# Decay attention in two sub-chunks of 64 tokens: every attention product as 64x64 tiles of the array

## The chip, the cores and the metric

The kernel runs on one core of one Trainium2 chip. The metric is the time of one execution on the device in microseconds (us), the median of several. The engines are named as in the profile: PE is TensorE (its weight loads are PEld), DVE is VectorE, ACT is ScalarE, POOL is GpSimd, SP is SyncE, which here only issues DMAs.

## The reference

Attention with a decaying state, then two feed-forward layers; all inputs are float32, and only the attention matters here.

```python
def _attn_ref(q, k, v, lam):          # q, k, v: 2 x 8 heads x 768 tokens x 64
    block = 64
    Dmask = np.where(rel >= 0, lam[:, None, None] ** rel[None, :, :], 0.0)
    for b in range(nb):
        intra = np.einsum('bhic,bhjc->bhij', qb, kb) * Dmask[None]
        intra = np.einsum('bhij,bhjd->bhid', intra, vb)
        inter = np.einsum('bhid,bhde->bhie', qb * lam_pow[None], kv_state)
        out[:, :, sl] = intra + inter
        kb_dec = kb * rev_pow[None]
        kv_state = lam_block[None, :, None, None] * kv_state + np.einsum('bhsd,bhse->bhde', kb_dec, vb)
...
x = moe(silu(x @ w_gate) * (x @ w_val) @ w_out);  return (g(x @ w_in)) @ w_out2   # 1536 tokens, g(h) = h cos h
```

The block of 64 is a way to compute, not part of the result: with the right powers of lam any block length gives the same numbers.

## The kernel before

A **chunk** is 128 tokens of one batch row with all eight heads; there are 12 (`NCH`), six for each of the two batch rows. Each chunk goes through these steps, which the PE executes in a written order (`steps_of`), mixed with feed-forward work:

- `t`: q and k are transposed on the PE (line 881), four 128x128 products each, and copied by ACT to `qt` and `kt`. The q side is multiplied by powers of lam on POOL to `qd`.
- `s`: the scores (line 895), eight products of 64 rows, 128x128 results. DVE multiplies them by the table `dmask` to `at`.
- `st`: the chunk's share of the state (line 902), eight products over 128 tokens with 64x64 results. DVE adds it to the old state, which POOL has multiplied by a power of lam (`stmp`).
- `av`: scores by values (line 908), eight products over 128 tokens with 64x128 results.
- `qs`: `qd` by the state (line 917), eight 64x64 weights against 128 columns, added into the same PSUM banks as `av`. ACT and DVE turn the sum into `xh` and `xl`, the input of the first layer.

A product of float32 operands (all but `t`) is two MATMUL records in the profile. Line 243 multiplies zeros where the order expects the PE to wait. A **unit** is one product of the first layer for 512 tokens: twelve matmuls of 512 columns on lines 136 to 138. All the matmuls of the feed-forward layers use three terms of split operands (`wh`, `wl`; `xh`, `xl`), for which DVE and ACT convert each loaded weight piece.

No order is left to the hardware: while the program is built, a small planner plays all engines with times written in the kernel (`ATT_NS`, the nanoseconds in `go(...)`), and emits each engine's instructions in the order in which they came up. An engine then executes its list strictly in order. The attention is the first part of the program; `FILL` says in how many places of it the planner should reckon with a unit. When the last chunk's `x` is there, DVE computes sums of `x` blocks (`t1`, `t2`, ..., `u1`, ...) that later products need (Strassen-like products of half blocks). DMAs of q, k, v and of weight pieces are all issued by SP, in the planner's order; a tile has 2 to 5 buffers (`BUFS`), and a load waits until its buffer is free.

Of the kernel before, what the change touches and what calls it, by code (L numbers as in the profile page):

```python
# [9 lines left out]
F32 = mybir.dt.float32  # L10
# [44 lines left out]
def kernel(  # L55
# [25 lines left out]
    C = P  # L81
    NPAIR = H // 2
# [115 lines left out]
    down_d = dram.tile([H, 2 * C], F32, name="down_d")  # L198
    down = att.tile([H, 2 * C], F32, name="down")
    anti = att.tile([P, P], F32, name="anti")  # L200
    dmask = att.tile([P, H, C], F32, name="dmask")
    zeros = att.tile([P, 512], mybir.dt.bfloat16, name="zeros")
    sel = s_tile(0, "sel")[0:H]
    lrow = att.tile([P, NPAIR, C], F32, name="lrow")
    state = [att.tile([P, NPAIR, D], F32, name=f"state{i}") for i in range(2)]

    def att_tile(nm, i):

        shape = {"q": [P, H, D], "k": [P, H, D], "v": [P, H, D], "kd": [P, H, D], "at": [P, H, C], "stmp": [P, NPAIR, D]}
        return att.tile(shape.get(nm, [P, NPAIR, C]), F32, tag=f"{nm}{i}", name=nm)  # L210

    def tables():
# [3 lines left out]
        nc.scalar.dma_start(down[:, C - 1:C], lam.rearrange("(h o) -> h o", o=1))  # L216
        nc.scalar.activation(warm, halfpi, AF.Silu)
        nc.vector.memset(down[:, C + 1:], 0.0)
        nc.vector.memset(down[:, C:C + 1], 1.0)
        n = 1  # L220
        while n < C:
            nc.vector.tensor_scalar(
                out=down[:, C - 2 * n:C - n], in0=down[:, C - n:C],
                scalar1=down[:, C - n:C - n + 1], scalar2=None, op0=ALU.mult,
            )
            n *= 2
        nc.scalar.dma_start(down_d, down)

    def load_mask():

        e = down_d[:, :]
        nc.sync.dma_start(dmask, bass.AP(e.tensor, e.offset + 1, [[1, P], [2 * C, H], [1, C]]))
# [13 lines left out]
    for g in range(NCH):  # L246
        if g % CPB != CPB - 1:
            steps_of.append(("st", g))
        steps_of.append(("av", g))
        if g % CPB:  # L250
            steps_of.append(("qs", g))
        if not g:
            steps_of += [("t", "q", 2), ("t", "k", 2)]
        if g + 2 < NCH:
            steps_of.append(("s", g + 2))
        if g + 3 < NCH:
            steps_of += [("t", "q", g + 3), ("t", "k", g + 3)]
        steps_of += [None] * FILL[g]
# [345 lines left out]
    def fetch(key, i):  # L604

        yield go("SP", 2300 if key[0] in up_w else 1700, lambda: load_piece(key, i))
# [145 lines left out]
    def qkv_job(nm, g):  # L752
# [6 lines left out]
        yield go("SP", 1330, lambda: nc.sync.dma_start(t, src[b, :, c * C:(c + 1) * C, :].rearrange("h p d -> p h d")))  # L759
# [7 lines left out]
    def t_copy_job(nm, g, b, ps):  # L767
# [7 lines left out]
        if nm == "q" and g % CPB:  # L775
# [3 lines left out]
            yield tt(qd[:, :, ::-1], t, lrow, ALU.mult, "POOL")  # L779
# [15 lines left out]
    readers = {}  # L795

    def done(nm, g, t):

        n = readers[nm, g] = readers.get((nm, g), 0) + 1
        if n == (2 if nm in ("k", "v", "qt") and (nm == "qt" and g % CPB or nm != "qt" and g % CPB != CPB - 1) else 1):  # L800
            give(nm, made_att.pop((nm, g))[0], t)

    def tmp_job(g):

        yield "wait", ("state", g)
        i = yield "take", "stmp"
        t = att_tile("stmp", i)
        yield tt(t, state[g % 2], lrow[:, :, 0:1].to_broadcast([P, NPAIR, D]), ALU.mult, "POOL")
        made_att["stmp", g] = i, t
        signal(("stmp", g), (yield "now",))  # L810

    def state_job(g, b, ps):

        pv = ps[:, 0:NPAIR * D].rearrange("p (a e) -> p a e", a=NPAIR)
        new = state[(g + 1) % 2]
        if g % CPB > 1 or g % CPB == 0 and g:
            yield "wait", ("qs", g - 1)
        if g % CPB:
            yield "wait", ("stmp", g)
            yield tt(new, made_att["stmp", g][1], pv, ALU.add, psum=True)  # L820
            done("stmp", g, (yield "now",))
# [3 lines left out]
        signal(("state", g + 1), (yield "now",))  # L825
# [583 lines left out]
```

## Time and profile before

| | |
|---|---|
| median of 3 runs | 597.47 us (597.45 to 597.63) |
| the profiled execution's span | 595.7 us |
| what lies around the span (median less span) | 1.8 us |
| PE busy / DVE busy / ACT busy / POOL busy | 589.6 / 500.8 / 347.9 / 30.5 us |
| attention | from the start to 80.65 us, with 7 units in it |

The span is the time from the first to the last instruction of one profiled execution; the timed runs have no profile and lie 1.8 us above it. The busy time of PE counts overlapping matmuls once, so a PE that is "busy" may still be waiting for its own pipeline: the starts of the groups tell more than their durations.

### The profile page before, as it was taken

How to read it: one execution, taken by the hardware profiler on the slowest of the kernel's cores; microseconds unless marked ns; L12 is line 12 of the kernel's file. 1: busy time of each engine (PE TensorE's matmuls, PEld its weight loads, DVE VectorE, ACT ScalarE, POOL GpSimd, SP SyncE). 2: the span in 40 equal slices, each digit the busy share in tenths (PEclk: the TensorE clock that was granted, in tenths of full speed). 3: DMA queues.
4: the chain of work that ended last, by engine and by line, in shares of the span. 5: the costliest groups of instructions: out<-in, count | busy, mean ns of one | idle time of the engine just before them, and what ended most of it. 6: DMA issues, size and time to landing. Idle time of an engine off the chain costs nothing.

```text
span 595.7 us, 8964 instructions
## 1 busy us (share of the span) xinstructions
PE 589.6 (99%) x3356; PEld 488.4 (82%) x3358; DVE 500.8 (84%) x885; ACT 347.9 (58%) x626; POOL 30.5 (5%) x37
## 2 busy tenths in 40 slices
PE   8999999999999999999999999999999999999997
PEld 5878878888888888888888878888888888888886
DVE  3568789999788788786889999999898999998854
ACT  2455455676656455544543776988666676676620
POOL 3634200000000000000000000000000000000000
PEclk9999999999999999999999999999999999999999
DMA  9999832058536537334322120110101222200005
GB/s 184 204 205 195 197 83 70 2 159 245 165 120 161 150 115 161 126 90 139 105 84 76 37 70 19 53 56 33 31 6 40 69 69 73 70 1 1 0 1 211
DMA packets 70570, 57.72 MB, mean 97 GB/s; under 512 B 39672, under 2 KB 61440, under 8 KB 70528
## 3 DMA queue, kind: packets, MB, share of 16 engines
q1 hardware_dynamic: 70496, 57.16, 36.7%
q8 instruction: 26, 0.43, 0.3%
q14 instruction: 16, 0.13, 0.1%
q10 hardware_dynamic: 32, 0.01, 0.0%
HBM read 49.81 MB, written 7.35 MB: 96 GB/s over the span
## 4 chain that ended last, share of the span: by engine, by line
PE 96%; DVE 3%; ACT 0%; issue 0%; DVEq 0%; ACTq 0%
PE bank L136 24%; PE bank L138 23%; PE bank L137 23%; PE bank L1237 5%; PE bank L1238 5%; PE bank L1239 5%; PE bank L895 2%; PE bank L881 2%; PE bank L908 2%; PE bank L243 1%; PE bank L902 1%; PE bank L917 1%; DVE sum L486 1%; DVE s L486 0%; DVE wl L498 0%
## 5 line engine op out<-in xcount | busy, mean ns | idle before, releaser
L136 PE MATMUL bank<-xl,wh 128*128 128x512 f32 (+1 forms) x336 | 123.5, 368 | 0.0
L137 PE MATMUL bank<-xh,wh 128*128 128x512 f32 (+1 forms) x336 | 122.6, 365 | 0.0
L138 PE MATMUL bank<-xh,wl 128*128 128x512 f32 (+1 forms) x336 | 122.3, 364 | 0.0
L493 ACT ACTIVATE s<-s 128x512 f32<-128x512 f32 (+2 forms) x112 | 65.8, 592 | 47.2 <-DVE s L486 27.4
L493 ACT ACTIVATE s<-bank 128x512 f32<-128x512 f32 (+2 forms) x114 | 61.2, 538 | 52.7 <-PE bank L138 47.3
L493 ACT ACTIVATE gh<-s 128x512 fp32r<-128x512 f32 x84 | 52.8, 629 | 58.3 <-PE bank L1238 30.9
L498 DVE TENSOR_TENSOR wl<-ct,wh 128x512 fp32r<-128x512 f32 x104 | 71.6, 702 | 6.4 <-ACT wh L493 6.3
L493 ACT ACTIVATE wh<-ct 128x512 fp32r<-128x512 f32 x104 | 63.4, 625 | 19.9 <-DVE ct L187 16.2
L137 PE MATMUL bank<-wh,gh 128*128 128x512 f32 (+1 forms) x194 | 75.0, 387 | 0.0
L136 PE MATMUL bank<-wl,gh 128*128 128x512 f32 (+1 forms) x194 | 75.0, 387 | 0.0
L138 PE MATMUL bank<-wh,gl 128*128 128x512 f32 (+1 forms) x194 | 75.0, 387 | 0.0
L136 PEld LDWEIGHTS bank<-xl,wh 128*128 128x128 f32 x336 | 63.3, 188 | 12.0 <-issue 0.7
L486 DVE TENSOR_TENSOR sum<-bank,sum 128x512 f32<-128x512 f32 (+1 forms) x101 | 65.1, 680 | 8.6 <-PE bank L138 7.8
L138 PEld LDWEIGHTS bank<-xh,wl 128*128 128x128 f32 x336 | 63.3, 188 | 10.3
L137 PEld LDWEIGHTS bank<-xh,wh 128*128 128x128 f32 x336 | 63.4, 189 | 10.1
L486 DVE TENSOR_TENSOR gl<-s,gh 128x512 fp32r<-128x512 f32 x84 | 57.8, 689 | 10.5 <-ACT gh L493 10.5
L486 DVE TENSOR_TENSOR s<-bank,s 128x512 f32<-128x512 f32 (+1 forms) x84 | 49.3, 591 | 16.7 <-PE bank L138 16.2
L1238 PE MATMUL bank<-gh,wh 128*128 128x512 f32 x144 | 56.3, 391 | 0.0
L1237 PE MATMUL bank<-gh,wl 128*128 128x512 f32 x144 | 56.3, 391 | 0.0
L1239 PE MATMUL bank<-gl,wh 128*128 128x512 f32 x144 | 56.0, 389 | 0.0
L187 DVE SCALAR_TENSOR_TENSOR ct<-ct,raw 128x512 int32<-128x512 int32 x68 | 46.8, 688 | 3.3 <-ACT ct L175 0.2
L175 ACT ACTIVATE ct<-raw 128x512 f32<-128x512 f32 x68 | 44.8, 663 | 3.7 <-DMA raw<-in_moe_w_out_dram 1.1
(122 smaller groups left out, 950.8 us busy)
## 6 DMA issues: line engine op xcount, KB each, us to landing
raw<-in_moe_w_out_dram SPq DMA_DIRECT2D x28, 512.0 KB, 3.6
raw<-in_moe_w_in_dram SPq DMA_DIRECT2D x16, 512.0 KB, 3.9
raw<-in_moe_w_gate_dram SPq DMA_DIRECT2D x24, 256.0 KB, 4.2
raw<-in_moe_w_val_dram SPq DMA_DIRECT2D x24, 256.0 KB, 4.3
q<-in_q_dram SPq DMA_DIRECT2D x12, 256.0 KB, 5.7
k<-in_k_dram SPq DMA_DIRECT2D x12, 256.0 KB, 5.5
v<-in_v_dram SPq DMA_DIRECT2D x12, 256.0 KB, 5.2
out_dram<-sum SPq DMA_DIRECT2D x11, 256.0 KB, 2.0
```

The lines of the kernel that those rows point to most:

```text
L136: nc.tensor.matmul(ps, wh, xl, start=first, stop=False, **kw)
L137: nc.tensor.matmul(ps, wh, xh, start=False, stop=False, **kw)
L138: nc.tensor.matmul(ps, wl, xh, start=False, stop=last, **kw)
L175: nc.scalar.activation(t, words[:, :, 1].bitcast(F32), AF.Prelu, scale=2.0 ** -112, alpha=2.0 ** 32)
L187: nc.vector.scalar_tensor_tensor(out=w, in0=w, scalar=3, in1=lo, op0=ALU.logical_shift_left, op1=ALU.bitwise_or)
L486: engine, n * (1.18 if engine == "DVE" else 2.45), lambda: unit.tensor_tensor(out=out, in0=in0, in1=in1, op=op),
L493: return go("ACT", 40 + n * 0.94, lambda: nc.scalar.activation(out, src, fn, **kw))
L498: return "any", {"DVE": n * 1.18, "POOL": n * 2.45}, lambda e: (nc.vector if e == "DVE" else nc.gpsimd).tensor_tensor(out=out, in0=in0, in ...
L881: nc.tensor.transpose(ps[:, p * P:(p + 1) * P], src[:, 2 * p:2 * p + 2, :].rearrange("p a d -> p (a d)"), anti if op[1] == "q" else ident,)
L1237: nc.tensor.matmul(ps, lo[:, cs], gh, start=first, stop=False)
L1238: nc.tensor.matmul(ps, hi[:, cs], gh, start=False, stop=False)
L1239: nc.tensor.matmul(ps, hi[:, cs], gl, start=False, stop=last)
```

## The change

A chunk stays 128 tokens for loads, transpositions and the output, but is computed in two sub-chunks `u` of 64 tokens (`CS`). The scores are only computed within a sub-chunk (64x64 results, two to a head), `dmask` and `at` are half as wide. The state is advanced twice a chunk (`st` makes two shares from 64 tokens each, with four state buffers), `qs` is two steps with a state each, and `av` is two steps: in the first each half of the array's rows writes one of the two output banks, in the second the other, with a `drain` of the PE ahead of the second. All of `s`, `st`, `av` and `qs` use 64x64 tiles of the array with 64 columns. The planner's times are changed with it, also those of the loads.

```diff
-ATT_NS = {"t": 480, "spread": 1080, "s": 1100, "st": 530, "av": 1080, "qs": 600}
+ATT_NS = {"t": 520, "spread": 400, "s": 540, "st": 530, "av": 270, "qs": 270}
-BUFS = {"q": 3, "k": 3, "v": 5, "qt": 2, "kt": 2, "qd": 3, "kd": 2, "at": 2, "stmp": 2}
+BUFS = {"q": 3, "k": 3, "v": 5, "qt": 2, "kt": 2, "qd": 3, "kd": 2, "at": 3, "stmp": 2}
+STATES = 4
+DRAIN = 150
...
     for g in range(NCH):
-        if g % CPB != CPB - 1:
-            steps_of.append(("st", g))
-        steps_of.append(("av", g))
-        if g % CPB:
-            steps_of.append(("qs", g))
...
+        steps_of.append(("st", g))
+        if g and g + 1 < NCH:
+            steps_of.append(("s", g + 1))
+        steps_of.append(("av", 0, g))
+        ahead = [2, 3] if not g else [g + 3] if g + 3 < NCH else []
+        steps_of += [("t", "q", n) for n in ahead]
+        steps_of += [("t", "k", n) for n in ahead]
+        steps_of += [None] * FILL[g]
+        steps_of.append(("av", 1, g))
...
-        yield go("SP", 2300 if key[0] in up_w else 1700, lambda: load_piece(key, i))
+        yield go("SP", 1800 if key[0] in up_w else 1700, lambda: load_piece(key, i))
...
-                    for h2, (_, ps) in enumerate(got):
-                        r = slice(64 * h2, 64 * h2 + 64)
-                        nc.tensor.matmul(ps[:, p * C:(p + 1) * C], kt[r, p, :], qt[r, p, :], start=True, stop=True)
+                    for h2 in range(2):
+                        for u in range(2):
+                            nc.tensor.matmul(
+                                got[h2][1][half(u), p * CS:(p + 1) * CS], kt[half(h2), p, half(u)], qt[half(h2), p, half(1 - u)],
+                                start=True, stop=True, skip_group_check=True,
+                            )
...
+                if turn:
+                    nc.tensor.drain()
...
+                for y in range(2):
+                    for u in range(2):
+                        for c in range(2):
+                            f = u ^ 1 ^ turn
+                            h = 2 * (2 * c + y) + f
+                            nc.tensor.matmul(
+                                put(made_att["out", g], f, c, y, u), vn[half(u), h, :], at_[half(u), h, :],
+                                start=not y and not turn, stop=turn == 1, skip_group_check=True,
+                            )
```

How this moves the PE's instructions: first a chunk of the middle of the attention before, where `bank2` and `bank4` are the output banks of chunk 7; steps come as `st`, `av`, `s`, `qs`.

```order
L902 MATMUL bank1_814<-v_414,kd_601 64x64 x8
L908 MATMUL bank2_825<-at_684,v_414 64x128 x4
L908 MATMUL bank4_826<-at_684,v_414 64x128 x4
L895 MATMUL bank5_840<-qt_776,kt_784 128x128
L895 MATMUL bank6_841<-qt_776,kt_784 128x128
```

The same part of the PE's list now, from the last scores of chunk 7 to the second half of `av` of chunk 6 (line 918 is `s`, 943 `av`, 904 `t`; `q_657` and `k_789` are the q and k of chunk 9):

```order
L918 MATMUL bank3_974<-qt_784,kt_795 64x64 x2
L918 MATMUL bank1_975<-qt_784,kt_795 64x64 x2
L943 MATMUL bank5_998<-at_860,v_424 64x64 x2
L943 MATMUL bank6_997<-at_860,v_424 64x64 x2
L904 MATMUL bank0_1010<-anti_89,q_657 128x128 x4
L904 MATMUL bank3_1018<-ident_84,k_789 128x128 x4
L943 MATMUL bank6_997<-at_860,v_424 64x64 x2
L943 MATMUL bank5_998<-at_860,v_424 64x64 x2
```

Every step is of 64x64 tiles, and the transpositions of chunk 9 stand between the two halves of one `av`, directly behind one another.

SP's list of loads, before, from the fifth to the twelfth (`v_142` is the v of chunk 0, `q_146` the q of chunk 2):

```order
L759 DMA v_142<-in_v_dram 128x8x64
L232 DMA dmask_90<-down_d_87 128x8x128
L759 DMA q_146<-in_q_dram 128x8x64
L759 DMA k_147<-in_k_dram 128x8x64
L759 DMA q_161<-in_q_dram 128x8x64
L759 DMA v_145<-in_v_dram 128x8x64
```

And now, from the v of chunk 0 (`v_143`) on, then behind the "..." the loads up to the k of chunk 9:

```order
L765 DMA v_143<-in_v_dram 128x8x64
L765 DMA q_147<-in_q_dram 128x8x64
L236 DMA dmask_90<-down_d_87 64x8x64 x2
L765 DMA q_162<-in_q_dram 128x8x64
...
L765 DMA k_678<-in_k_dram 128x8x64
L765 DMA v_424<-in_v_dram 128x8x64
L765 DMA q_657<-in_q_dram 128x8x64
L157 DMA raw_897<-in_moe_w_val_dram 64x4x256 x2
L765 DMA k_789<-in_k_dram 128x8x64
```

The load of `dmask` (512 KB before, now two of 128 KB) has one more q ahead of it. The four first weight pieces all stand ahead of the k of chunk 9; three did before.

The end of the attention on the PE, before: `av` of chunk 11, a unit (its twelve matmuls go on behind the "..."), `qs`, and the next unit.

```order
L908 MATMUL bank2_1130<-at_1011,v_747 64x128 x4
L136 MATMUL bank0_1144<-xl_135,wh_719 128x512
...
L917 MATMUL bank6_1129<-qd_950,state1_95 64x128
...
L136 MATMUL bank5_1178<-xl_135,wh_811 128x512
```

The unit of `bank0_1144` is the seventh. Now:

```order
L943 MATMUL bank4_1552<-at_1464,v_1038 64x64 x2
L139 MATMUL bank0_1607<-xl_136,wh_1095 128x512
...
L952 MATMUL bank3_1551<-qd_1335,state2_96 64x64 x2
...
L139 MATMUL bank6_1688<-xl_138,wh_595 128x512
```

Here the unit of `bank0_1607` is the eighth: one unit more stands ahead of the last `qs`, and one fewer behind it. Behind that the lists of the feed-forward layers are nearly the same.

## Rows read from the trace of the kernel before

**Rows 1.** The page: busy time and share; the chain that ended last, by engine.

```profile
PE 589.6 (99%) x3356; PEld 488.4 (82%) x3358; DVE 500.8 (84%) x885; ACT 347.9 (58%) x626; POOL 30.5 (5%) x37
...
PE 96%; DVE 3%; ACT 0%; issue 0%; DVEq 0%; ACTq 0%
```

**Rows 2.** Stretches, core 0: length, busy by engine, clock, DMA share, GB/s.

```profile
core 0: us, PE busy (x) PEld busy (x) DVE busy (x) ACT busy (x) POOL busy (x), PEclk, DMA share, GB/s
5.00:63.00 58.00, 57.20 (x719) 45.26 (x720) 34.55 (x63) 25.84 (x53) 27.36 (x27) 1.00 1.11 204
...
90.00:105.00 15.00, 15.00 (x71) 12.53 (x70) 14.70 (x19) 8.39 (x13) 0.00 (x0) 1.00 0.28 70
105.00:120.00 15.00, 15.00 (x82) 12.95 (x81) 14.52 (x26) 10.11 (x20) 0.00 (x0) 1.00 0.01 2
```

**Rows 3.** Waits of PE, 5.7 to 80.7 us: total, times, longest.

```profile
PE bank L895 <- ACT kt L493: 0.6, 2, 0.3
```

**Rows 4.** Timeline of PE, middle of the attention: start, length, line, operands, count.

```profile
39.52 0.66 PE L881 MATMUL bank<-anti,q 128*128 128x128 f32 x4
40.11 1.09 PE L908 MATMUL bank<-at,v 128*64 128x128 f32 x16
41.13 0.66 PE L881 MATMUL bank<-ident,k 128*128 128x128 f32 x4
41.72 0.67 PE L917 MATMUL bank<-qd,state 64*64 64x128 f32 x16
42.32 0.66 PE L881 MATMUL bank<-anti,q 128*128 128x128 f32 x4
42.91 1.16 PE L895 MATMUL bank<-qt,kt 64*128 64x128 f32 x16
44.00 0.66 PE L881 MATMUL bank<-ident,k 128*128 128x128 f32 x4
...
47.33 0.69 PE L902 MATMUL bank<-v,kd 128*64 128x64 f32 x16
47.84 1.05 PE L908 MATMUL bank<-at,v 128*64 128x128 f32 x16
48.82 1.16 PE L895 MATMUL bank<-qt,kt 64*128 64x128 f32 x16
49.91 0.66 PE L881 MATMUL bank<-anti,q 128*128 128x128 f32 x4
50.40 0.60 PE L881 MATMUL bank<-ident,k 128*128 128x128 f32 x4
```

**Rows 5.** One stretch of 0.045 us, line 917 alone: PE busy and records, clock, DMA.

```profile
41.70:41.74 0.04, 0.02 (x4) 1.00 1.20 250
```

**Rows 6.** Timeline of PE: a run of zeros.

```profile
12.53 1.90 PE L243 MATMUL bank<-zeros 128*128 128x512 bf16 x8
14.27 0.60 PE L881 MATMUL bank<-anti,q 128*128 128x128 f32 x4
```

**Rows 7.** Timeline of SP: start and length of a DMA's issue.

```profile
3.70 1.14 SPq L759 DMA_DIRECT2D v<-in_v_dram  x1
7.78 0.37 SPq L232 DMA_DIRECT2D dmask<-down_d  x1
...
41.26 3.13 SPq L759 DMA_DIRECT2D k<-in_k_dram  x1
```

**Rows 8.** Timeline, end of the attention.

```profile
77.11 0.50 PE L136 MATMUL bank<-xl,wh 128*128 128x512 f32 x1
...
80.05 0.67 PE L917 MATMUL bank<-qd,state 64*64 64x128 f32 x16
...
80.65 0.50 PE L136 MATMUL bank<-xl,wh 128*128 128x512 f32 x1
...
81.19 0.76 DVE L486 TENSOR_TENSOR xl<-bank,xh 128x256 fp32r<-128x256 f32 x2
```

**Rows 9.** Timeline behind the attention: a sum's low half, and its first use.

```profile
101.67 1.22 DVE L486 TENSOR_TENSOR t2l<-sum,t2h 128x1024 fp32r<-128x1024 f32 x1
...
103.96 0.39 PE L136 MATMUL bank<-t2l,wh 128*128 128x512 f32 x1
```

**Rows 10.** Groups of POOL and DVE, 0 to 120 us: busy, mean ns | idle before.

```profile
L486 POOL TENSOR_TENSOR qd<-qt,lrow 128x512 f32<-128x512 f32 x10 | 12.9, 1294 | 24.1 <-ACT qt L493 24.1
L486 POOL TENSOR_TENSOR kd<-k,dmask 128x512 f32<-128x512 f32 x10 | 10.5, 1058 | 9.1 <-issue 4.9 <-DMA k<-in_k_dram 3.0 <-DMA dmask<-down_d 1.3
L486 POOL TENSOR_TENSOR stmp<-state,lrow 128x256 f32<-128x256 f32 x8 | 5.9, 733 | 2.4 <-DVE state L486 2.4
```

More of the change, by code (lines that the diff above doesn't have):

```diff
@@ L81 @@
     C = P
+    CS = C // 2
     NPAIR = H // 2
@@ L824, in state_job @@
         drop_bank(b, (yield "now",))
-        signal(("state", g + 1), (yield "now",))
+        signal(("state", n + 1), (yield "now",))
     def at_job(g, got):
@@ L903, in fn @@
             elif kind == "av":
                 at_, vn = made_att["at", g][1], made_att["v", g][1]
-                made_att["out", g] = list(got)
-                for f in range(2):
-                    for a in (0, 2, 1, 3):
-                        nc.tensor.matmul(
-                            put(got, f, a), vn[:, 2 * a + f, :], at_[:, 2 * a + f, :],
-                            start=a % 2 == 0, stop=not g % CPB and a % 2 == 1, skip_group_check=True,
-                        )
+                turn = op[1]
@@ new lines, in fn @@
+                if turn:
+                    nc.tensor.drain()
+                else:
+                    made_att["out", g] = list(got)
+                for y in range(2):
+                    for u in range(2):
+                        for c in range(2):
+                            f = u ^ 1 ^ turn
+                            h = 2 * (2 * c + y) + f
+                            nc.tensor.matmul(
+                                put(made_att["out", g], f, c, y, u), vn[half(u), h, :], at_[half(u), h, :],
+                                start=not y and not turn, stop=turn == 1, skip_group_check=True,
+                            )
@@ L912, in fn @@
             else:
-                out_, qd = made_att["out", g], made_att["qd", g][1]
+                out_, qd, u = made_att["out", g], made_att["qd", g][1], op[1]
                 for y in range(2):
-                    for f, a in ((0, y), (1, y + 2), (0, y + 2), (1, y)):
-                        r = slice(64 * f, 64 * f + 64)
-                        nc.tensor.matmul(
-                            put(out_, f, a), state[g % 2][r, a, :], qd[r, a, :], start=False, stop=y == 1, skip_group_check=True
-                        )
+                    for f in range(2):
+                        for c in range(2):
+                            nc.tensor.matmul(
+                                put(out_, f, c, y, u), state_of(2 * g + u)[half(f), 2 * c + y, :], qd[half(f), 2 * c + y, half(u)],
+                                start=False, stop=y == 1, skip_group_check=True,
+                            )
@@ L935, in then @@
             else:
-                signal((kind, g), t)
-                if kind == "av":
+                signal(op, t)
+                if kind == "qs":
+                    done("qd", g, t)
+                elif op[1]:
                     done("at", g, t)
                     done("v", g, t)
-                else:
-                    done("qd", g, t)
-                if kind == "qs" or not g % CPB:
+                if kind == "qs" and op[1]:
                     for f, (b, ps) in enumerate(made_att["out", g]):
                         spawn(out_job(g, f, b, ps), seen[op], t)
-        return dict(ns=ATT_NS[kind], needs=needs, keys=[], bank=n, fn=fn, then=then, clock=seen[op], op=op)
+        return dict(ns=ATT_NS[kind] + DRAIN * (op[:2] == ("av", 1)), needs=needs, keys=[], bank=n, fn=fn, then=then, clock=seen[op], op=op)
     def open_mlp(t):
@@ L1366 @@
             for nm in "qkv":
[L1367 removed]
+                spawn(qkv_job(nm, g), seen["t", "q", g] if nm == "q" else seen["t", "k", g] if nm == "k" else seen["av", 0, g] - 1)
         spawn(mask_job(), seen["s", 0], 6500)
         for g in range(NCH):
[L1370 to L1373 removed]
+            spawn(kd_job(g), seen["st", g] - 2)
+            for n in (2 * g, 2 * g + 1):
+                if n % (2 * CPB) and not ends(n):
+                    spawn(tmp_job(n), seen["st", g] - 1)
         spawn(y_job(), 0)
```

114 lines of the change are left out of this document (60 added, 54 removed).

## The prediction, made before the changed kernel had run

> **What bounds the kernel now.** I read the page first: PE is busy in 99% of the span, and 96% of the chain that ended last is PE [rows 1]. So time is won only where the PE's own list gets shorter, and kept only if nothing else makes it wait. Then the waits of PE in the attention: 0.6 us in all, none for a DMA [rows 3]. But the stretches show two neighbours that have almost no room. From 5 to 63 us the DMA engines move 204 GB/s without a break [rows 2], and SP is held up while issuing: 3.13 us for one load of k [rows 7]. Behind the attention DVE is busy for 29.2 of the 30 us from 90 to 120 [rows 2], and its results are ready just ahead of their use: the low half of `t2` ends at 102.89 (101.67 + 1.22), and the PE takes it at 103.96, 1.07 us later [rows 9].
>
> **What a step costs on the PE.** In the timeline [rows 4] I take the time from one group's start to the next one's. `t` with a second `t` behind it lasts 0.49 (49.91 to 50.40), with another tile shape behind it 0.59 (39.52 to 40.11): leaving a shape costs 0.10. `av` behind `st` of the same shape: 0.98 (47.84 to 48.82), less 0.10 to leave, is 0.88 for eight steps, 0.110 each, where a step is the two matmuls in different tiles that run together with 128 columns. With that, four products of `t` leave 0.05 of the 0.49 for entering the shape. `st`, with 64 columns, lasts 0.51 (47.33 to 47.84): 0.05 and eight steps of 0.058. `qs` uses 64x64 tiles: 0.60 (41.72 to 42.32) is 0.15 for entering and leaving and four steps of about 0.11, now with four matmuls in each.
>
> **The array's own saving.** A product of float32 is two records, so per chunk before: `s` 8 steps, `av` 8, `st` 8 (ten chunks), `qs` 4 (ten chunks). In all (96 + 96 + 40) x 0.110 + 80 x 0.058 = 30.2 us. Now all is in steps of four tiles with 64 columns: `s` 96, `av` 96, `st` 88, `qs` 88, 368 steps. The trace shows four tiles only with 128 columns, and 64 columns only in pairs. Nearest below is the pair of `st`, 0.058; nearest above the four of `qs`, 0.11. I take 0.058, since 128 columns cost the same 0.11 in twos and in fours: the number of tiles costs nothing there, the columns do. 368 x 0.058 = 21.3, 8.9 less. Changes of shape, counted in the two lists up to the last `qs`: 61 before, 47 now, as `av`, `qs`, `st` and `s` share a shape; 14 x 0.15 = 2.1 less. Zeros: 16 instead of 14 at 0.217 (1.74 for eight [rows 6]), 0.4 more; the product that spreads the powers has half the columns and gives about that back. The twelve drains: seven stand behind a `t` or a unit, where the shape changes anyway; five stand between two halves of `av`. The trace has no drain. It costs from nothing to the whole length of a matmul, 0.27 (the last of four in the 0.60 of the `t` at 50.40, less three steps of 0.11 [rows 4]); I take a change of shape, 0.15, so 0.8. Sum: 8.9 + 2.1 - 0.8 = about 10.2 us of PE time.
>
> **What the loads give back.** The array can't run ahead of its data. Before, the k of chunk 9 is transposed at 50.40 [rows 4]. Now the two transpositions of chunk 9 stand directly behind one another, and everything behind them on PE waits: 156 of the 368 steps, six units. In SP's list that load is now the 36th of 256 KB (a weight piece counts two; before it was the 35th, with `dmask` as two). 36 x 0.262 MB at 204 GB/s [rows 2] is 46.3 us; SP's first issues and the wait for `dmask`, of which before shows 2.9 us (4.84 to 7.78 [rows 7]) and of which one q now fills 1.2, put some 2.2 on it: about 48.5. Ends: 46.5 without any of that, 50.4 as before. Without it PE would be there at about 45 (212 of the 368 steps are done, 212/368 x 10.2 = 5.9 less than 50.40, give or take the changed order), so it waits about 3.5.
> From there on, all in the PE's list: 156 x 0.058 = 9.0; five transpositions 5 x 0.44 = 2.2; six units of twelve matmuls, 6 x 2.75 = 16.5 (2.93 from 77.11 to 80.05 with its change of shape [rows 8]); 13 changes 1.95; two drains 0.3: 30.0. With 0.5 for the v of chunk 7, which lands just behind, and 0.2 for the landing to be seen: the last `qs` ends at 48.5 + 0.2 + 30.0 + 0.5 = 79.2. Before it ended at 80.65 [rows 8], but with seven units ahead of it, now eight: 83.6 is what 79.2 stands against. Gain on PE: 4.4.
>
> **What DVE gives back.** It starts on the sums when the last `x` is there: 81.95 before (81.19 + 0.76 [rows 8], 1.3 behind `qs`), 80.5 now, only 1.45 earlier, as the eighth unit is ahead of it. PE wants `t2` 4.4 earlier, and had 1.07 in hand: if DVE's list behind that point is as long as before, PE waits 4.4 - 1.45 - 1.07 = 1.9. If it is shorter by what the eighth unit's result needs on DVE (a multiplication or a split, 0.7 each), it waits 0.5. I take about 1.0. On DVE itself `at` halves and the state is added twice as often, which nearly cancels and is hidden in the attention, where DVE is busy for 34.6 of 58 us [rows 2]; were it not, it would cost some 2 us.
> Sum: 4.4 - 1.0 = 3.4, so 594.0 from the median of 597.47; in the profiled span 595.7 becomes 592.3, the 1.8 us around it stay.
>
> **Rivals.** *The loads don't hold the array up*: the k of chunk 9 lands by 45, as the DMA engines have no pauses any more, and PE keeps the 10.2, less 1 to 2 that DVE takes back as above. That is 588.3. For it: before, no PE wait is for a DMA [rows 3]. Against it: 204 GB/s is held for 58 us already.
> *Nothing is left*: POOL sets the pace. For a chunk it now has 1.29 (`qd`) + 1.06 (`kd`) + 2 x 0.73 (`stmp`) = 3.81 us [rows 10], in one queue, where it had 3.1. In the stretches without units the PE needs about 3.2 a chunk. If six chunks go at POOL's pace, 6 x 0.6 = 3.6 are gone: 597.6. Against it: there the loads (3 x 1.28 = 3.9 a chunk at 204 GB/s) are slower than POOL anyway.
> *Slower*: steps of four tiles don't get shorter with the columns. At 0.110 instead of 0.058 the 368 steps cost 19.1 more; 10.2 - 19.1 is 8.9 lost, 606.4. It decides from 0.067 a step, where 368 x 0.009 eats the 3.4. For it: no row shows four tiles at 64 columns, and a step would hold four starts and four weight loads. Against it: in one window of `qs` four matmuls start within 25 ns (41.72 to 41.745 [rows 5]), so eight such issues would still fit into 58.
> The Trainium skill (TensorE: Matmul & The Clock Gate, section "Wait — 56ns, not 53.3ns?") says that matmul starts are never closer than about 25 ns, however few the columns. By that rule four starts would take 0.10, and this rival would hold, at about 604. The trace differs: four within 25 ns, so I give it no more than the rival's chance.
>
> **How the numbers follow.** What a measurement of this kernel can tell from no change is about 0.2%, 1.2 us. The likeliest case, 594.0: 0.56, from 590.5 (k of chunk 9 at 46.5, DVE nothing) to 596.3 (at 50, DVE 1.9). No loads in the way, under 590.5: 0.17. Nothing left, 596.3 to 598.7: 0.12. Slower: 0.15. So faster 0.73, same 0.12, slower 0.15. The range 588.3 to 598.5 leaves out the slower cases and the better half of the second, about 2 in 10.
>
> **What the profile will show.** Groups of `s` and `st` of about 0.6 with 32 records each, 58 ns between steps; a wait of PE for a DMA of k or q at about 45 to 48.5 us; the last `qs` ending at about 79; then a PE wait on a DVE result at 100 to 120. I am wrong if a step of four tiles takes more than 65 ns; if the PE is not waiting ahead of the k of chunk 9; if a wait for the `drain` is longer than 0.3 a time; or if the long wait lets the granted clock fall from the 1.00 that all stretches show [rows 2], which would make the matmuls behind it slower for a time.

## The result and the profile after

The changed kernel takes 604.58 us (median of four runs, 602.82 to 605.14), the kernel before 597.55 beside it: ratio 1.0112, 95% interval 1.0098 to 1.0127, about 7 us slower. The profiled execution is the fastest of the four: span 601.0, 5.3 longer than before; its mean granted clock is 0.996, that of the other three 0.991 to 0.993.

From the page: busy time, the chain, the queue that brings PE's instructions. Against [rows 1], PE is busy for 4 us less and the span is longer, so PE waits; "issue", 0% of the chain before, has 2% of it. (PE's matmuls rise from 3356 to 4128, the packets on q8 from 26 to 32. With weight loads, drains and semaphore instructions PE has 6763 records before and 8308 now, which is 26.4 and 32.5 times 256.)

```profile
PE 585.5 (97%) x4128; PEld 484.2 (81%) x4128; DVE 495.8 (82%) x894; ACT 349.2 (58%) x626; POOL 45.1 (8%) x55
...
q8 instruction: 32, 0.52, 0.4%
...
PE 93%; DVE 4%; issue 2%; ACT 0%; DVEq 0%
```

The stretch of [rows 2], 5 to 63 us: PE is busy for 49.8 us where it was for 57.2, with more than the 719 records it had there.

```profile
5.00:63.00 58.00, 49.82 (x1230) 38.20 (x1232) 28.02 (x63) 24.38 (x49) 32.90 (x34) 0.97 1.07 203
```

Waits of PE in the attention, 5.7 to 90 us, beside 0.6 in [rows 3]. Six rows are "issue": PE waits though no semaphore that the profile shows is late.

```profile
PE bank L139 <- DVE xl L492: 1.9, 2, 0.9
PE bank L141 <- issue: 1.8, 1, 1.8
PE bank L943 <- issue: 1.5, 1, 1.5
PE bank L952 <- issue: 0.9, 1, 0.9
PE bank L904 <- issue: 0.8, 1, 0.8
PE bank L918 <- issue: 0.7, 1, 0.7
PE bank L952 <- DVE state L492: 0.5, 1, 0.5
PE bank L927 <- issue: 0.3, 1, 0.3
```

Three of them in PE's timeline. They stand in the middle of a group, where all operands are there: between the second and the third matmul of a unit, and behind 20 of the 32 records of `av`.

```profile
26.18 0.45 PE L952 MATMUL bank<-qd,state 64*64 64x64 f32 x12 [0.50 <-DVE state L492]
27.53 0.27 PE L952 MATMUL bank<-qd,state 64*64 64x64 f32 x2 [0.90 <-issue]
...
43.58 0.40 PE L140 MATMUL bank<-xh,wh 128*128 128x512 f32 x1
45.77 0.50 PE L141 MATMUL bank<-xh,wl 128*128 128x512 f32 x1 [1.79 <-issue]
...
47.11 0.63 PE L140 MATMUL bank<-xh,wh 128*128 128x512 f32 x1
47.54 0.63 PE L141 MATMUL bank<-xh,wl 128*128 128x512 f32 x1
...
57.35 0.39 PE L943 MATMUL bank<-at,v 64*64 64x64 f32 x10 [1.54 <-issue]
```

What sets their places is seen by counting. Here are stretches that each begin at 0 and end where such a wait ends; the first two counts in brackets are PE's matmuls and weight loads so far.

```profile
0.00:21.80 21.80, 19.68 (x346) 12.43 (x347) 6.09 (x22) 7.52 (x13) 12.67 (x20) 1.00 1.04 194
0.00:27.52 27.52, 23.77 (x473) 15.57 (x474) 10.38 (x31) 10.45 (x19) 16.55 (x24) 1.00 1.05 192
0.00:32.74 32.74, 28.06 (x599) 18.86 (x600) 13.63 (x37) 12.54 (x23) 20.07 (x28) 1.00 1.05 195
0.00:45.76 45.76, 38.15 (x852) 26.72 (x852) 21.19 (x54) 19.14 (x36) 26.61 (x35) 1.00 1.05 197
0.00:57.34 57.34, 47.98 (x1104) 34.71 (x1105) 28.31 (x70) 23.63 (x46) 32.18 (x41) 0.97 1.03 195
0.00:69.45 69.45, 59.32 (x1357) 44.16 (x1357) 33.68 (x82) 28.68 (x56) 39.52 (x49) 0.98 1.01 195
```

Their sums are 693, 947, 1199, 1704, 2209 and 2714: from wait to wait 254, 252, 505, 505, 505. With the drains and semaphore instructions that the trace also records for PE, the first new record is number 705, 961, 1217, 1729, 2241 and 2753, counted from 0: the distances are 256, 256, 512, 512, 512. Queue q8 brings packets of 16384 bytes, 256 times 64. The table sets these blocks of 256 against the packets (times from the trace's records; the last column is the gap between two starts):

| first record | block before it began | its packet on the DMA engines | it began | gap |
|---|---|---|---|---|
| 705 | 17.39 | 19.15 to 20.50 | 21.81 | 0.56 |
| 961 | 21.81 | 24.80 to 26.12 | 27.53 | 1.12 |
| 1217 | 27.53 | 30.00 to 31.24 | 32.74 | 1.09 |
| 1473 | 32.74 | 33.91 to 35.26 | 40.19 | - |
| 1729 | 40.19 | 42.62 to 43.89 | 45.77 | 2.19 |
| 2241 | 52.05 | 54.60 to 55.92 | 57.35 | 1.76 |
| 2753 | 62.86 | 67.15 to 68.31 | 69.45 | 0.88 |

PE's instructions come in blocks of 256, and in the attention the packet of a block starts only when PE has begun the one before it. Where PE stood, the block was used 1.1 to 1.9 us behind its landing and 4.4 to 6.6 us behind the start of the block before. In the kernel before, blocks of the attention lasted 7 to 12 us, and none was late; now a group of 64 such instructions takes 0.47 us, and a chunk has 272 where it had 144. The gaps sum to 7.6 us, of which some 7.2 are lost: without a wait the matmul of the unit would follow in 0.23 us (46.11 to 46.34 in the trace), the others in at most 0.06.

The Trainium skill (Runtime: NRT & Kernel Launch, section "Instruction fetch mechanics") states the block of 16 KiB and 256 instructions, and that crossing its boundary is mostly hidden. The trace agrees on the block; in this kernel a crossing opens a gap of up to 2.19 us between two starts.

Behind the 1.79 us the granted clock fell to 0.50, that is to 1.2 GHz, and matmuls started 0.43 us apart (47.11 to 47.54):

```profile
46.94:50.35 3.41, 3.41 (x15) 2.39 (x17) 0.87 (x2) 0.00 (x0) 0.00 (x0) 0.50 1.15 197
```

The end of the attention, which answers to [rows 8]: the last `qs` starts at 86.74, and the ninth unit, at 83.50 before, at 88.36, behind a wait for the last `x`.

```profile
86.74 0.69 PE L952 MATMUL bank<-qd,state 64*64 64x64 f32 x32
88.36 0.50 PE L139 MATMUL bank<-xl,wh 128*128 128x512 f32 x1 [0.93 <-DVE xl L492]
```

PE's time from 4.6 us to the ninth unit by kind, worked out from the records (from each matmul's start to the next one's, less what the trace calls idle), in us:

| | `s` | `av` | `st` | `qs` | all four | `t`, zeros, units | idle |
|---|---|---|---|---|---|---|---|
| before | 13.1 | 11.9 | 5.4 | 6.0 | 36.3 | 41.8 | 0.8 |
| changed | 6.7 | 9.0 | 6.3 | 6.8 | 28.9 | 44.7 | 10.2 |

The products became 7.5 us shorter. The third group (`t`, zeros, units) grew by 3.0, of which about 1.7, half of 3.41, is the stretch at the low clock. Idle time grew by 9.4, of which 6.0 are "issue". The sum (all before rounding) is the 4.9 by which the ninth unit is later, and nearly all of the 5.3 of the span.

### The profile page after: what moved, and what is told of

Same layout as the page of the kernel before. It is cut to its first block, busy times and chain, and to the rows that moved or that the text cites. A ratio compares the mean times of both kernels' runs of the same rounds, so it can differ in the third digit from the quotient of the medians.

```text
span 601.0 us, 10527 instructions
## 1 busy us (share of the span) xinstructions
PE 585.5 (97%) x4128; PEld 484.2 (81%) x4128; DVE 495.8 (82%) x894; ACT 349.2 (58%) x626; POOL 45.1 (8%) x55
## 4 chain that ended last, share of the span: by engine, by line
PE 93%; DVE 4%; issue 2%; ACT 0%; DVEq 0%
PE bank L139 24%; PE bank L141 23%; PE bank L140 23%; PE bank L1274 5%; PE bank L1275 5%; PE bank L1276 5%; PE bank L904 2%; PE bank L943 1%; PE bank L249 1%; PE bank L927 1%; PE bank L952 1%; PE bank L918 1%; DVE s L492 1%; DVE sum L492 1%; DVE xl L492 1%
```

## The experiments

Theory A: PE's instruction blocks come late. Theory B, the rival: the waits are those of the new order of steps, of x, of banks, or of the state's chain on POOL and DVE. Each ratio is against the kernel before, with its 95% interval.

**Zeros (e10_zeros).** If PE stands still for want of instructions, work of few instructions costs little.

```diff
             if kind == "t":
+                zero(ps, 2 if g > 2 else 0)
```

> The changed kernel with two more products of zeros (512 columns, 0.217 us, two instructions each) ahead of every t of chunks 3 to 11: 36 of them, 7.8 us of array time, 72 instructions. Theory A: PE stands still for 7.6 us because instructions are late, and work of few instructions fits into that time: the waits at multiples of 256 records fall by 3 to 6 us and the time rises only by 1.5 to 4.5, 606 to 609. If the array itself sets the pace: the time rises by all 7.8, 612.

605.07 us, 1.0117 (1.0091 to 1.0144): 7.8 us more of array work for 0.5, less even than the 1.5 to 4.5 that Theory A expected. The waits for "issue":

```profile
PE bank L944 <- issue: 1.5, 2, 0.8
PE bank L928 <- issue: 0.3, 1, 0.3
```

The gaps at block boundaries fall from 7.6 to 2.8 (0.5, 0.3, 1.0 and 0.9), and the mean clock is 1.00, so a part of the 7.8 is paid by the fall of the clock that doesn't happen. The array doesn't set the pace.

**Small zeros (e16_small_zeros).** The same zeros with eight times the instructions.

```diff
-                zero(ps, 2 if g > 2 else 0)
+                for _ in range(16 if g > 2 else 0):
+                    nc.tensor.matmul(ps[:, 0:64], zeros[:, 0:P], zeros[:, 0:64], start=True, stop=True)
```

> The run with zeros again, but each of its 36 zero products of 512 columns is cut into eight of 64 columns: the same columns to stream, 576 instructions in place of 72, so a chunk has some 330 PE instructions. Theory A: 504 instructions are two blocks of 256 at 5.2 to 5.6 us each, of which the longer blocks take up 2 to 4: 6 to 9 us more than the run with zeros (605.1), 611 to 614, with waits over 0.5 us at more multiples of 256 records than its three. If only streamed columns count: 604 to 607. If a small zero product takes longer than its 64 columns (over 0.04 us each), the t groups get longer evenly and the time with them, and the run tells nothing of the blocks.

612.44 us, 1.0263 (1.0227 to 1.0299): 7.4 more than with large zeros, inside Theory A's 6 to 9. Sixteen small zeros take 0.48 us (71.54 to 72.02), two large ones 0.44 (62.98 to 63.42): 18 such runs differ by 0.7 us, not by 7.4.

```profile
71.54 0.64 PE L903 MATMUL bank<-zeros 128*128 128x64 bf16 x16
72.02 0.63 PE L906 MATMUL bank<-anti,q 128*128 128x128 f32 x4
```

```profile
62.98 0.60 PE L249 MATMUL bank<-zeros 128*128 128x512 bf16 x2
63.42 0.60 PE L905 MATMUL bank<-anti,q 128*128 128x128 f32 x4
```

And a run of zeros, which needs no data, now stops after twelve of sixteen; record 2753 is the next one:

```profile
61.31 0.52 PE L903 MATMUL bank<-zeros 128*128 128x64 bf16 x12
64.01 0.29 PE L903 MATMUL bank<-zeros 128*128 128x64 bf16 x4 [2.17 <-issue]
```

So 504 instructions cost 7.4 us, 14.6 ns each. The two profiled executions are 8.5 us apart: five late blocks with gaps of 1.7, 1.1, 0.9, 0.7 and 2.4 us make 3.9 more than the four with large zeros, two stretches of 3.41 us at a clock of 0.50, behind the first and the last of the five, cost about half their length, 3.4, and the zeros themselves 0.7. This is the clearest evidence for Theory A.

**Old loads (e8_old_loads).** The planner's times of the loads as before.

```diff
-        yield go("SP", 1150, lambda: nc.sync.dma_start(t, src[b, :, ...
+        yield go("SP", 1330, lambda: nc.sync.dma_start(t, src[b, :, ...
-        yield go("SP", 1800 if key[0] in up_w else 1700, ...
+        yield go("SP", 2300 if key[0] in up_w else 1700, ...
```

> The changed kernel with the planner's times for the loads as in the kernel before, nothing else. Theory A: the same number of PE instructions, so 603 to 606, with waits again 256 records apart. Theory B with the loads as the cause (the new times of the loads put q, k, v and weights in a worse order): the loss goes, 595 to 599.

603.09, 1.0083 (1.0066 to 1.0101). The loss stays. PE's order is another, and yet it stands at such records again: 449, 705, 961, 1985 and 2753, for 0.5, 1.0, 2.2, 2.4 and 1.2 us.

**Shared loads (e5_shared_loads), and the same on the kernel before (e15_before_shared).** A chunk of odd number reads the tiles of the chunk before it.

```diff
+        if g % 2:
+            t = tile_of[nm, g - 1]
...
+            yield go("SP", 1150, lambda: None)
```

> The changed kernel with half of the q, k and v loads left out: a chunk of odd number reads the q, k and v of the chunk before it (its results are those of that chunk's data). PE's list, all its 256-instruction blocks, the steps, copies and the order on every engine stay as they were; only the DMA engines have 18 loads of 0.26 MB less, so that they move about 125 instead of 203 GB/s to 58 us. Theory A (instruction blocks come late because their 16 KB packets wait among the data loads): the packets start sooner (the wait from the start of one block to the start of the next packet, 1.2 to 4.3 us now, falls to about 1), the waits at records 705, 961, 1217, 1729, 2241 and 2753, now 7.6 us in sum, fall to 0 to 3, and the time to 594 to 599. Theory A without the load (a block takes 5 us from order to use whatever the other queues do): the waits stay where they are, 601 to 604. Theory B (order of steps, x, banks, the state chain on POOL and DVE): nothing of it is touched, 602 to 605.

> The kernel before with the shared loads, as a control: in it PE waits for no load and no block, so that taking half of the q, k and v loads away gives nothing: 596.5 to 598.5. A gain of over 1 us would say that lighter loads help whatever the instructions do, and that the gain of the shared loads in the changed kernel (604.6 to 600.1) is no sign of late blocks.

The kernel before doesn't gain: 597.37, 0.9995 (0.9987 to 1.0004). The changed kernel comes to 600.13, 1.0035 (1.0015 to 1.0054), 596.1 to 602.5 from run to run. It missed the range of Theory A by a little: the loads moved forward, so that the DMA engines were still full in places. In the profiled execution (602.5, the slowest of the ten) blocks are late at 32.67, 51.59 and 56.09, by 2.6, 0.7 and 1.7 us; in the light stretches, 36 to 44 and 57 to 78, none is:

```profile
28.00:36.00 8.00, 4.63 (x106) 3.67 (x95) 3.31 (x9) 2.61 (x6) 3.96 (x5) 0.78 1.04 189
36.00:44.00 8.00, 7.89 (x179) 6.41 (x178) 2.64 (x6) 2.81 (x6) 3.14 (x4) 0.79 0.31 68
44.00:57.00 13.00, 10.83 (x314) 8.88 (x307) 10.60 (x24) 6.58 (x14) 8.43 (x10) 1.00 0.83 185
57.00:78.00 21.00, 20.68 (x496) 17.03 (x494) 13.28 (x30) 9.36 (x21) 11.78 (x14) 1.00 0.18 53
```

From 57 to 78 packets start 0.65 to 1.9 us behind the beginning of the block before, against 1.2 to 4.3 between 17 and 75 in the changed kernel. The data loads are part of a block's delay.

**Wide tiles (e1_wide), tall tiles (e9_tall, e12_tall_banks).** Half of the instructions for equal array work was the aim. For `s`:

```diff
-                        for u in range(2):
-                            nc.tensor.matmul(
-                                got[h2][1][half(u), p * CS:(p + 1) * CS], kt[half(h2), p, half(u)], qt[half(h2), p, half(1 - u)],
+                        nc.tensor.matmul(
+                            got[h2][1][:, p * CS:(p + 1) * CS], kt[half(h2), p, :], qt[half(h2), p, half(1)],
```

> The changed kernel with each pair of 64x64 products of s, st, av and qs replaced by one product that fills 64 rows by 128 columns of the array and streams 64 columns: 368 of its 736 attention products are left out (half of the results are those of a neighbouring head or sub-chunk), the groups still make eight steps each, and loads, copies, DVE and POOL work and the order are as they were. PE's list gets 1472 instructions shorter. Theory A (PE's instructions come by DMA in blocks of 256, and a block takes 5.2 to 6.6 us from the moment the one before it is begun, while data loads fill the DMA engines): without half of the instructions a block holds two chunks, no wait stands at a multiple of 256 records any more, the last qs ends near 80 us, and the time is 594 to 597 us. Theory B (the waits are those of the new order of steps, of x, of banks or of the state chain on POOL and DVE): these depend on what was left untouched, so the time stays at 602 to 605. If a weight load of 128 columns can't hide behind 64 streamed ones, steps last 0.11 us instead of 0.058 and the time is above 605 without any wait at multiples of 256.

611.16, 1.0234 (1.0217 to 1.0251). No gap is left at a block boundary, idle time up to the ninth unit is 3.1 us instead of 10.2. But a step takes 0.11 us, though it streams 64 columns: eight steps of `s` last 0.94 with entering the shape (25.16 to 26.10), and 0.89 behind a group of the same shape. The four products together grow by 17.7 us, and the time by 6.6. Of the 11 us that don't show, 7.1 are the idle time, and 2.9 the rest of the list, which runs at full clock; the last 1 is not accounted for.

The tall tiles leave the weights 64 columns wide:

```diff
-                                got[u][1][half(h2), p * D:(p + 1) * D], kd[half(u), 2 * p + h2, :], vn[half(u), 2 * p + h2, :],
+                            ps[half(h2), p * D:(p + 1) * D], kd[:, 2 * p + h2, :], vn[:, 2 * p + h2, :],
...
-                    nc.tensor.drain()
...
+                            made_att["out", g][turn][1][half(c), y * C:y * C + C], vn[:, h + turn, :],
+                            at_[:, h:h + 2, :].rearrange("p a i -> p (a i)"), start=not y, stop=y == 1, skip_group_check=True,
```

> The changed kernel with st and av in tiles of 128 rows by 64 columns, which take the same time on the array with half the instructions: st makes its first share over all 128 tokens of the chunk and the second state reads that share too (the second share is left out), av multiplies all 128 tokens in one product of 128 columns (scores of two heads stand where those of one head's sub-chunk should be), without the drain. Per chunk 8 st products of 64 columns in place of 16, 0.467 us as now, and 8 av products of 128 columns, 0.88, as now 0.85 with its drain; DVE, POOL, ACT, the loads and the order stay. PE has 752 instructions less. Theory A (instruction blocks): the waits of 7.6 us at multiples of 256 records shrink to 0 to 3, the clock doesn't fall, and the time is 596 to 600 (up to 2 us of it are given back by changes of tile shape, 0.15 each). Theory B (order, x, banks, the state chain): array time, order and data are the same, so 603 to 606.

608.83, 1.0174 (1.0152 to 1.0195): no late block, but PE waits 5.6 us for DVE's state, for a bank that this edit hands on too early. Mended:

> The run with tiles of 128 rows, mended: there the second state read the bank of the first, which was handed on after the first had been read, so that PE waited 5.6 us for DVE's state in three places, a wait of that edit. Now the two banks of st change places when they are given back. Theory A (the late instruction blocks are the loss): no wait stands at a multiple of 256 records, those three waits are gone too, and the time is 597 to 601.5. Theory C (behind the late blocks stand the loads and the state chain, which hold PE up as much as soon as its instructions come in time): other waits of 4 us or more take their place, and the time stays at 602.5 to 606.

601.40, 1.0068 (1.0053 to 1.0082), 3.2 less than the changed kernel. Theories A and C are each half right. No block is late, but now the loads are, as the prediction had it, among them the k of chunk 9:

```profile
50.13 0.66 PE L904 MATMUL bank<-anti,q 128*128 128x128 f32 x4
52.81 0.41 PE L904 MATMUL bank<-ident,k 128*128 128x128 f32 x2 [2.02 <-DMA k<-in_k_dram]
```

```profile
PE bank L904 <- DMA k<-in_k_dram: 2.7, 2, 2.0
PE bank L139 <- DVE xl L492: 1.9, 2, 0.9
PE bank L904 <- DMA q<-in_q_dram: 1.6, 1, 1.6
PE bank L904 <- ACT ct L178: 1.6, 1, 1.6
```

That the tall tiles "take the same time on the array with half the instructions" (e9_tall) did not hold: the four products take 34.1 us here, 5.2 more than in the changed kernel, as `av` takes 12.9 instead of 9.0.

**Both edits (e14_both).**

> Both edits in one: the tiles of 128 rows (half of the instructions of st and av, the same array time) and the shared loads (18 of the 36 q, k and v loads left out). If instruction blocks and loads are the two limits, one behind the other, PE now has neither: no wait at multiples of 256 records, none for a DMA, the last qs with eight units ahead of it ends at 78 to 82, and the time is 589 to 595. If the chain over DVE and POOL, or the array, holds PE at the same pace, the time stays at 599 to 602, as with either edit alone.

599.92, 1.0040 (1.0026 to 1.0054). Idle time falls to 2.75 us, 1.9 of it for `x`, 0.6 for one late block (record 1729, though none was expected), and the last `qs`, from 81.49, ends at about 82, as expected; but the time misses the range and lies in the rival's, 599 to 602. With the longer `av` PE's list from 5 us to the ninth unit is only 2.3 us shorter than before (75.4 against 77.7), and the ninth unit starts at 83.11 instead of 83.50. Yet the profiled span, 596.9, is 1.2 longer than before: 1.6 us are lost behind the ninth unit. A wait of 1.0 us for DVE at 151 us, which the kernel before doesn't have, is a part of them; the rest is open.

**Another form of av (e13_diag).** All products, but `av` over 128 tokens with zeros beside the two blocks of scores.

```diff
+                            made_att["out", g][turn][1][half(c), y * C:y * C + C], vn[:, h, :], at_[:, h, :],
...
+            for u in range(2):
+                r = slice(CS * u, CS * u + CS)
+                yield tt(
+                    at_[r, h2::2, r][:, :, ::-1], ps[r, 0:NPAIR * CS].rearrange("p (a i) -> p a i", a=NPAIR), dmask[r, h2::2, :],
```

> All products of the changed kernel, but av in one form with fewer instructions: the scores of the two sub-chunks are written by DVE into the two diagonal blocks of a 128x128 tile whose other blocks were set to zero once, so av is again eight products over 128 tokens with 128 columns (0.88 us, 32 instructions less a chunk, no drain), for four DVE instructions of half the rows in place of two (0.83 us a chunk more on DVE). 384 PE instructions less than the changed kernel. Theory A: the waits at multiples of 256 records, 7.6 us there, shrink to under 4, and the time is 599 to 602, between the two kernels. Theory C: DVE's and the loads' waits fill up what is gained: 603 to 606. If it beats both kernels, under 596.5, halving one of the four products is the better cut of this work.

The edit also changes three numbers of the planner (`av` 440 instead of 270, `DRAIN` 0 instead of 150, two buffers for `at` instead of three), so the lists of the other engines aren't those of the changed kernel.

606.23, 1.0146 (1.0125 to 1.0167), no gain: blocks are late by 6.3 us in sum, against under 4 expected, and the longer `av` is paid for.

**Other places of the units (e6_paced, e7_paced_old_loads, e11_unit_early).** Only numbers of the planner: step times of 21 ns an instruction, or units one chunk earlier.

```diff
-ATT_NS = {"t": 520, "spread": 400, "s": 540, "st": 530, "av": 270, "qs": 270}
+ATT_NS = {"t": 520, "spread": 400, "s": 1340, "st": 1340, "av": 670, "qs": 670}
-FILL = (0, 0, 0, 0, 0, 1, 1, 1, 1, 1, 1, 1)
+FILL = (0, 0, 0, 0, 1, 1, 1, 1, 1, 1, 1, 1)
```

> The changed kernel with other numbers for the planner alone: it reckons with 21 ns for each PE instruction of a step (5.4 us for 256): s and st 1340 ns, av and qs 670 each, and with a unit from chunk 4 on, one a chunk. All products are there. The order that comes of it has a unit in nearly every block of 256 instructions from the fifth on, where the changed kernel has two blocks without one, which ran dry after 3.4 and 3.5 us. Theory A: the waits of 2.2 and 1.8 at records 1729 and 2241 go, and with them the fall of the clock behind the first; the waits ahead of the first x stay (about 3 to 6 us in sum), and the last qs ends, with eight units ahead of it, 3 to 5 us earlier than at 87.3: 599 to 602. Theory B (the waits come from the order of steps and from x): moving units changes which step waits, and the time goes either way by 2 us, 602 to 607, with waits not at multiples of 256.

> The paced kernel, with the planner's times for the loads as in the kernel before (1330 ns for q, k and v, 2300 for a weight piece). Theory A: within 1 us of the paced kernel, as the PE instructions and not the data set the pace: 599 to 602. If the order of loads matters: over 1.5 us apart from it.

> The changed kernel with the seven places of units in the planner's list one chunk earlier (from chunk 4 on), its step times as they were. The order that comes of it has a unit in the two blocks of 256 that ran dry after 3.4 and 3.5 us. Theory A, as far as the planner's other lists aren't disturbed (as they were with the paced times): the waits at records 1729 and 2241 (2.2 and 1.8) shrink by half or more, and the time falls by 1 to 4 us, 600.5 to 603.5. If it only moves the waits: 604 to 605.

618.83, 617.62 and 611.47 us: all three expectations failed. In the paced kernel PE waits in other places, 5.7 and 4.5 us for DVE's state and 3.5 for `s`, DVE's result of a unit; with units earlier, packets start up to 6.8 us behind the beginning of the block before, and the gaps at boundaries grow to 9.8. One number of the planner moves the lists of all engines and the loads; these runs say nothing about the places of the units alone.

**Two drains (e4_two_drains).** A second `nc.tensor.drain()` behind the first.

> The changed kernel with two drains in place of one ahead of the second turn of av. The trace shows five places where the two turns of av are neighbours, and there the drain costs 0.38 us. Theory A and B alike: the second drain finds the array empty; if it costs as much again, 5 times 0.38 plus 7 times 0.1 to 0.38 behind other work, 2.6 to 4.6 us more (607 to 609); if only the emptying costs, under 0.05 each and no difference (604 to 605).

604.50, 1.0118 (1.0098 to 1.0137): the time shows no second price. The trace shows a small one: the two halves of `av` back to back, with `qs` behind them, take 0.93 us instead of 0.85 at full clock. So the second drain costs 0.08 where the first costs 0.38; twelve times 0.08 is below what these runs can tell.

**Extra instructions on the kernel before (e2_sem4, e3_ld4).** Four behind each attention product.

```diff
+            for _ in range(4):
+                nc.tensor.sem_inc(pads[0], 1)
```

> The kernel before, with four extra instructions on PE's queue behind each attention product, each adding 1 to a semaphore that nobody reads: 1408 more, so that a chunk has as many PE instructions as in the changed kernel, with nothing else moved. Theory A: the attention then holds about 13 blocks of 256 in some 70 us, 5.4 us each, so part of them come late: waits of 0.5 to 2 us at equal distances in PE's list, 1.2 to 1.9 us behind the landing of a 16 KB instruction packet, and a time 2 to 8 us longer, 600 to 606. Theory B: the order and the data are those of before, so no such waits and 597.5 to 599. If one such instruction holds the queue up by more than 14 ns, the eight of a step take longer than the step's 0.11 us, and the groups get longer evenly, whichever theory holds.

> The same as the run with semaphore instructions, but the four extra instructions behind each attention product are weight loads of 64x64 zeros in bfloat16 that the next product's own weight load overwrites. Theory A: 600 to 606 with waits of 0.5 to 2 us every 256 records of PE (these weight loads do stand in the records). Theory B: 597.5 to 600, without such waits. If the array can't hide these loads, the groups get longer evenly, by up to 1408 times the 7 to 30 ns of one, 10 to 40 us, whichever theory holds.

757.67 and 816.30 us (one run each): 0.11 and 0.16 us for each extra instruction, evenly spread and without any wait at boundaries, since blocks became that much longer. The clock, whose mean fell to 0.886 and 0.857, is in these numbers. At full clock a product and its four extra instructions last 0.60 us with semaphore instructions (`av`, 27.48 to 28.09 in the trace) and 0.46 with weight loads (`st`, 29.29 to 29.75), where a product alone lasts 0.11 and 0.058: some 0.12 and 0.10 each. They tell nothing about the theories; e16_small_zeros did what they were meant to.

## Why the prediction was wrong

It said 594.0 and faster; 604.6 came. First the lines of the changed kernel on which the answers rest: a group of `st` with `qs` behind it, the two halves of `av` back to back, and the transposition of the k of chunk 9.

```profile
16.97 0.65 PE L927 MATMUL bank<-v,kd 64*64 64x64 f32 x32
17.44 0.42 PE L952 MATMUL bank<-qd,state 64*64 64x64 f32 x16
...
19.11 1.03 PE L943 MATMUL bank<-at,v 64*64 64x64 f32 x32 [0.20 <-DVE xl L492]
19.96 0.42 PE L952 MATMUL bank<-qd,state 64*64 64x64 f32 x16
...
52.55 0.60 PE L904 MATMUL bank<-ident,k 128*128 128x128 f32 x4
```

By its steps:

- *What a step costs.* Right. Groups of four tiles with 64 columns follow each other at 0.467 us for eight steps (16.97 to 17.44), 0.058 each. The slower rival is refuted. The rule of the Trainium skill (TensorE: Matmul & The Clock Gate, section "Wait — 56ns, not 53.3ns?") that starts are never closer than about 25 ns doesn't hold here: four in 58 ns are 14.6 each. (By the prediction's own terms that rule gives about 603, not 604, and the lower end of its likeliest case is 591, not 590.5; neither moves the range.) The prediction's sentence that the number of tiles costs nothing and the columns do is too wide, though: with weights of 128 columns a step stays at 0.11 (e1_wide).
- *The array's own saving*, 10.2. The four products, with their changes of shape and drains, became 7.5 shorter. The drain was mis-sized: the two halves of `av` back to back take 0.85 us (19.11 to 19.96) instead of 0.467, five times 0.38 is 1.9, where 0.8 was put; 0.38 is also over the 0.3 that the prediction named as a sign of being wrong. The changes of shape, put at 2.1, gave less as well: if the steps gave their 8.9, about 0.5 is left for them in these groups (7.5 + 1.9 - 8.9), by an estimate from the table.
- *What the loads give back* is the step that failed. "Without it PE would be there at about 45" took for granted that the array's list is all that PE needs. The change doubles the instructions of the products, and they come by DMA too: where the prediction had a wait of 3.5 us for a load, PE had waited for its own instructions. The k of chunk 9 was transposed at 52.55 without a wait, because PE was late itself; up to there the late blocks had taken 5.0 us (0.56, 1.12, 1.09 and 2.19 of the table), the low clock 1.7 (half of 3.41) and the wait for `x` ahead of the first unit 0.94. Together 7.6 us, as much as 52.55 is later than 45, though that is rough: the 45 was, and 0.5 for the state and some drains stand there too. (In e14_both, with half of the loads gone and no block late up to there, PE was there at 47.00 without a wait, with the longer `av`.) Behind it two more late blocks (2.6) and the second wait for `x` (0.93) follow. The limit of the loads itself is real, and later than its 48.5: by the trace's records the k of chunk 9 landed at 50.30 in the changed kernel, and with the late blocks taken away (e12_tall_banks) at 52.67, where PE waits for it until 52.81.
- *What DVE gives back*, 1.0. Nothing could be given back in the changed kernel. Where PE came earlier, in e14_both, there was no wait between 100 and 120 us either: the low half of `t2` was ready at 103.57 and taken at 104.39. Its wait of 1.0 us for DVE, at 151 us, is another.
- *Rivals.* None had the supply of instructions, though the prediction counted two records to each product and the products go from 352 to 736. Its own sign, "if the PE is not waiting ahead of the k of chunk 9", showed that it was wrong, and the fall of the clock that it named came, but behind a wait for instructions.

How the 7 us divide can't be told to the last one: the late blocks and the waits behind them overlap with the loads, and the three executions that took longest have no trace. That the late blocks set the pace is shown by the two runs with zeros; that without them the loads take over, by e12_tall_banks. No run showed a version faster than the kernel before.

## What to carry to other kernels

Count PE's instructions beside the columns: smaller tiles that run together make the array faster, but each is a weight load and a matmul for every pass. Where a block of 256 PE instructions would last less than it takes from the start of one block to the first use of the next (4.4 to 6.6 us here, with data loads of about 200 GB/s beside it), expect PE to stand still at distances of 256 records, in the middle of groups and with "issue" as the releaser; work with few instructions fits in for nearly nothing there (7.8 us for 0.5 in e10_zeros). Before a gain on one engine is counted, ask of each of its supplies, the instructions too, how fast it can come.

## What the runs showed of the hardware

The 16 KB packet of a block takes 0.9 to 1.9 us on the DMA engines in the attention, and in no run did PE use it sooner than 1.1 us behind its landing. A drain between two groups of one tile shape costs 0.38 us, a second one behind it 0.08. A semaphore instruction on PE's queue costs about 0.12 us between small products (e2_sem4), and a weight load in bfloat16 between float32 products about 0.10 us (e3_ld4), both at full clock, far more than the 0.03 us of a small zero product among its like (e16_small_zeros). Four 64x64 tiles with 64 columns start every 58 ns; two tiles with weights of 128 columns start every 0.11 us, though they stream 64 columns as well (e1_wide).
